# Out products of two slices in one run, in the float32r layers of the groups of 448 columns

## The chip, the cores and the metric

The kernel runs on one core of one Trainium2 chip. The metric is the device time of one execution in microseconds (us), the median of several runs.

## The reference

Attention with a memory, then two gated feed-forward layers ("MoE" by their names, with a single expert). With B = 4, H = 8, S = 576, D = 64:

```python
local = softmax(causal(q @ k.T / sqrt(D))) @ v
mem   = (phi(q) @ M_prev) / (phi(q) @ z_prev + 1e-6)       # phi(x) = elu(x) + 1
x     = g * mem + (1 - g) * local                          # g = sigmoid(beta), by head
x     = x.reshape(B * S, 512)                              # 2304 tokens
xn    = x / sqrt(mean(x * x) + 1e-6) * rms_g
x1    = (silu(xn @ w_gate) * (xn @ w_val)) @ w_out         # 512 -> 1536 -> 512
out   = (sigmoid(x1 @ w_gate2) * (x1 @ w_val2)) @ w_out2
```

All is float32. The kernel reaches that precision by writing each operand as a high and a low part and adding three products (high by high, high by low, low by high).

## The kernel before

The tokens are worked in five groups: group -1 has the first 128 tokens of all four batches (512 columns), groups 0 to 3 have the other 448 tokens of one batch each (448 columns). Each group goes through both layers, l = 0 and l = 1. A layer is cut into 12 slices of 128 hidden units. For a slice f, `hidden` makes two sums in PSUM, `pg` (gate) and `pv` (value), with twelve matmuls each (line 961: four blocks of 128 by three products). `gated` turns them into the hidden values `h`: a tanh on ScalarE (line 981), then on VectorE lines 983 and 986 for a first layer or line 990 for a second, and a split into a high and a low part (lines 998 and 999, or 1005 and 1006). `out_share` multiplies `h` with the out weights into four accumulators `po` (line 1027), twelve matmuls again. `pg` and `pv` come from a pool of two PSUM buffers (`psm`), `h` from three buffers, and `po` stands in four banks for a whole layer.

In group 0 and up the products of `hidden` are made in 16-bit halves (f16), except in the first two slices of a second layer, which are float32r. The out products are float32r in both layers of group 0 and in the first layer of group 1, and f16 halves later on. The rows show float32r operands as f32.

Weights: SyncE loads them from copies kept in DRAM into a ring of thirteen buffers (`slot`; in the rows `ws`, `wl`, `wr`, `wrl`). In the layers of group 0 a slice takes three of them: one for the kept raw weights (line 915), one for their halves, which are made there (`halve`: lines 830 to 837 on ScalarE, GpSimd and VectorE), and one for the out weights (line 927). In group 1 the halves are loaded ready (line 903).

While a group's layers run, the attention of the next group is worked in between in small steps (`att_qk`, `att_scores`, `att_av`, `att_mem`, lines 210 to 638), and in group 1 also the halving of the out weights for later (`share_steps`). After the out products of each slice the loop sets out some of these steps. SyncE issues all loads and stores in one queue, in order; an instruction that waits there holds up those behind it.

The order on each engine is not that of the program: a planner (`schedule_with_timeline_sim=True`) goes through the instructions with priorities in program order and its own times, and gives each engine the next that it takes to be ready. Within an engine the chip then keeps to that order.

The part of the loop that matters here: `hidden(f)` comes first, and the out products of slice f-1 after it, so that `h` of f-1 has had the time of a slice to be made. `done` counts the steps and sets the pace of the attention work.

Of the kernel before, what the change touches and what calls it, by code (L numbers as in the profile page):

```python
# [68 lines left out]
def attn_moe_moe_kernel(ctx, tc, qT, kT, qk0, v, mz, beta, w8, rms_g, outT):  # L69
# [11 lines left out]
    NF = w8.shape[1]  # L81
# [884 lines left out]
    def hidden(w, l, f, n, g, x, h, o=0, home=("mm", "mm")):  # L966

        pool, tag = late[home[0]], home[1]
        pg = pool.tile([128, NMAX], F32, tag=tag, name="pg")
        mm3(pg, w[0], x, n, o)  # L970
        pv = pool.tile([128, NMAX], F32, tag=tag, name="pv")
        mm3(pv, w[1], x, n, o)

        gated(pg, pv, l, f, n, g, h, o)
# [35 lines left out]
    def htiles(g, l, f):  # L1010
        t = wp.tile([128, NMAX], F32, tag="t", bufs=3, name="t")
        if plain(g, l, f):
            return t, None
        if is_share(g, l, f):
            return t, late["h"].tile([128, 2, 2, NMAX], F16, tag="h", bufs=3, name="h")[:, 0]
        return t, late["h"].tile([128, 2, NMAX], F32R, tag="h", bufs=3, name="h")

    def out_share(w, h, po, n, first, last):
        t, hh = h
        low = 0 if hh is None or w[2].shape[1] < 3 else 2  # L1020
        for d in range(KD):
            c = slice(d * 128, (d + 1) * 128)
            if hh is None:
                nc.tensor.matmul(po[d][:, 0:n], w[2][:, c], t[:, 0:n], start=first, stop=last)
                continue
            for i, (a, b) in enumerate(((0, 0), (low, 1), (1, 0))):
                nc.tensor.matmul(  # L1027
                    po[d][:, 0:n], w[2][:, a, c], hh[:, b, 0:n], start=(first and i == 0), stop=(last and i == 2)
                )
# [3 lines left out]
    def token_sums(xh, tag):  # L1033

        t = xp.tile([128, 2, 4, NMAX], F16, tag=tag, name="t" + tag)
        halves = [t[:, a, :, 0:2 * NT].rearrange("p j (k n) -> p j k n", k=2) for a in range(2)]
        for k in range(2):
            x = ap_.tile([128, SW], F32, tag="pt", name="xw")[:, 0:4 * NT].rearrange("p (i n) -> p i n", i=2)
            nc.vector.tensor_tensor(
                out=x,  # L1040
                in0=xh[0].rearrange("p (i k) n -> p k i n", k=2)[:, k, :, 0:2 * NT],
                in1=xh[1].rearrange("p (i k) n -> p k i n", k=2)[:, k, :, 0:2 * NT],
                op=ALU.add,
            )
            part = lambda i, j: x[:, i, j * NT:(j + 1) * NT]
            tw = ap_.tile([128, SW], F32, tag="sc", bufs=2, name="tw")[:, 0:4 * NT].rearrange("p (j n) -> p j n", j=4)
            for j, (a, b) in enumerate(
                ((part(0, 1), part(0, 0)), (part(1, 1), tw[:, 0]), (part(1, 1), part(0, 1)), (tw[:, 1], part(1, 0)))
            ):
                nc.vector.tensor_tensor(out=tw[:, j], in0=a, in1=b, op=ALU.subtract)  # L1050
            nc.scalar.copy(out=halves[0][:, :, k], in_=tw)
            nc.vector.tensor_tensor(out=halves[1][:, :, k], in0=tw, in1=halves[0][:, :, k], op=ALU.subtract)
        return halves
# [301 lines left out]
    def last_of(e):  # L1355
        return next(i for i in reversed(nc.cur_bb.bb.instructions) if i.engine == e)

    def behind(pairs):

        stack = ExitStack()  # L1360
        for pair in pairs:
            for i in pair:
                stack.enter_context(tc.issue_after(i))
        return stack

    def lagged(n):

        return marks[-n:len(marks) - n + 1] if len(marks) >= n else []
# [18 lines left out]
    def unit_slices(g):  # L1387
        mid = NF if g < B - 1 else NF // 2 + 2
        for e, c in ((nc.vector, slice(NWIDE, mid)), (nc.gpsimd, slice(mid, NF))):
            if c.start < c.stop:  # L1390
                e.tensor_scalar(out=unit[2][:, c], in0=unit[1][:, c], scalar1=st["half_is1"], scalar2=None, op0=ALU.mult)
# [45 lines left out]
    for g in range(-1, B):  # L1437
        n = 512 if g < 0 else S - 128
# [16 lines left out]
        for l in range(2):  # L1455
            early = 2 if g < 0 and l == 0 else 0
            ws, hs, halfway = early_ws[:early], early_hs[:early], []
            for f in range(early):
                hidden(ws[f], l, f, 256, g, xt, hs[f], 256, (("mm", "mm"), ("ps", "pa"))[f])
                halfway.append(tuple(last_of(e) for e in (mybir.EngineType.Activation, mybir.EngineType.DVE)))  # L1460
            po = None
            if g == B - 1:
                po = [late[f"po{d // 2}"].tile([128, NMAX], F32, tag=f"po{d}", name="po") for d in range(KD)]
                halves = xt if l == 0 else xh
                xs = token_sums(halves, "c" if l == 0 else "a")
                last_slices(l, n, xt, halves, xs, po)
            for f in range(0 if g == B - 1 else NF + 1):
                if f < NF:
                    if f >= early:
                        if g > 0 and l == 1 and f == NWIDE:  # L1470
                            unit_slices(g)
                        turn = lagged(BACK[g + 1]) if g <= 0 else []
                        if g < 0 and l == 1 and f in (2,):
                            turn = turn + evacuated
                        if g >= 0 and l == 0 and f in (1, 2):
                            turn = turn + tokens_done
                        with behind(turn + (halfway[-1:] if early and f < early + 3 else [])):
                            ws.append(weights(g, l, f))
                        hs.append(htiles(g, l, f))
                        if g == B - 2 and l == 1 and f == NF - 3:  # L1480
                            first_sums(0)
                        hidden(ws[f], l, f, n, g, xh if l == 1 and is_half(g, l, f) else xt, hs[f])
                        marks.append(tuple(last_of(e) for e in (mybir.EngineType.Activation, mybir.EngineType.DVE)))
                if f > 0:
                    if po is None:
                        po = [late[f"po{d // 2}"].tile([128, NMAX], F32, tag=f"po{d}", name="po") for d in range(KD)]
                    out_share(ws[f - 1], hs[f - 1], po, n, f == 1, f == NF)
                    done += 1
                    with ExitStack() as after:

                        if g < 0 and done < 5:
                            traced = nc.cur_bb.bb.instructions
                            for e in (mybir.EngineType.Activation, mybir.EngineType.DVE, mybir.EngineType.SP):
                                after.enter_context(
                                    tc.issue_after(next(i for i in reversed(traced) if i.engine == e))
                                )
                        for step in shares[done]:
                            with behind(lagged(2)):
                                step()
                        while used < len(steps) and used < len(steps) * (done - wait) // (total - wait):  # L1500
                            with behind(lagged(AFTER[g + 1])):
                                steps[used]()
                            used += 1
                            if used == len(steps):
                                tokens_done = [tuple(last_of(e) for e in (mybir.EngineType.Activation, mybir.EngineType.DVE))]
            if g < 0 and l == 0:
                begin.close()
            xn = wide_tokens("cd") if l == 0 else None
            for d in range(KD):
                evacuate(l, d, n, g, po[d], xn)  # L1510
            evacuated = [tuple(last_of(e) for e in (mybir.EngineType.Activation, mybir.EngineType.DVE))]
            if l == 0 and g >= 0:
                xh = half_tokens("b")
                with tc.high_priority(400):
                    halve_tokens(g, n, po, xh)
                    if g >= NSHARE[1]:
                        group_unit()
            if l == 0 and g < 0:
                with tc.issue_after(z["gm"]):
                    token_scale()  # L1520
            xt = xn
# [56 lines left out]
```

## Time and profile before

| | |
|---|---|
| Median of three runs | 1014.85 us (1014.1 to 1015.68) |
| The profiled execution | 1016.42 us |
| Its span, first to last instruction | 1014.6 us |
| TensorE busy | 999.3 us (98%) |
| VectorE busy | 832.1 us (82%) |
| ScalarE busy | 654.7 us (65%) |
| Mean granted clock of TensorE | 0.996 of full speed |

Busy times are sums over the span. The ends of matmuls are modelled: a matmul of 448 columns shows some 0.35 us although one starts every 0.19 us, so the pace is read from one start to the next. PE is TensorE (PEld its weight loads), DVE VectorE, ACT ScalarE, POOL GpSimd, SPq the queue of SyncE. L1027 is line 1027 of the kernel. A granted clock of 1.00 is 2.4 GHz, 0.50 is 1.2 GHz.

### The profile page before, as it was taken

What the parts mean: (1) busy time and instruction counts of PE and PEld (TensorE: products, weight loads), DVE (VectorE), ACT (ScalarE), POOL (GpSimd) and SP (SyncE); (2) the same over time, 40 slices, a digit from 0 to 9 for tenths busy, and PEclk for the clock granted to TensorE, in tenths of its full rate; (3) what the DMA queues carried; (4) which work ended last, traced back from release to release, by engine and by line L of the source; (5) the groups of instructions that cost most, each with busy time, mean ns of one, the idle gap of its engine ahead of it and who ended that gap; (6) DMA issues with size and microseconds to landing.
All of it is one profiled execution on the core that took longest, in us unless ns stands there. A gap on an engine that the chain in (4) does not pass through costs nothing.

```text
span 1014.6 us, 19021 instructions
## 1 busy us (share of the span) xinstructions
PE 999.3 (98%) x6721; PEld 700.0 (69%) x6721; DVE 832.1 (82%) x1826; ACT 654.7 (65%) x1238; POOL 201.8 (20%) x339
## 2 busy tenths in 40 slices
PE   9999999999999999999999999999999999999998
PEld 6878887888666676666666765555567556876885
DVE  6989999997769998775998977757779776995883
ACT  7668887786678888674778676535456353543452
POOL 4203221141004233300424432002133100000000
PEclk9999999999999999999999999999999999999999
DMA  9599998986894676498779856995544256836521
GB/s 350 180 373 398 345 352 257 376 308 200 272 368 172 224 251 229 177 322 240 246 257 322 266 179 224 309 340 167 174 144 167 83 159 212 284 135 226 201 84 37
DMA packets 102561, 243.74 MB, mean 240 GB/s; under 512 B 25154, under 2 KB 37058, under 8 KB 102466
## 3 DMA queue, kind: packets, MB, share of 16 engines
q1 hardware_dynamic: 102322, 242.41, 69.8%
q8 instruction: 53, 0.87, 0.3%
q14 instruction: 42, 0.34, 0.1%
q10 hardware_dynamic: 144, 0.11, 0.0%
HBM read 187.43 MB, written 51.38 MB: 235 GB/s over the span
## 4 chain that ended last, share of the span: by engine, by line
PE 65%; DVE 14%; issue 9%; DMA 6%; ACT 5%; POOL 1%; SPq 0%; DVEq 0%; POOLq 0%; ACTq 0%
PE po L1027 20%; PE pg L961 16%; PE pv L961 15%; PE pw L1137 7%; PE ps L253 2%; DMA qd<-in_qT 1%; PE pm L638 1%; POOL sc L555 1%; DVE mx L572 1%; DMA raw<-in_w 1%; DMA wr<-kept 1%; PE pav L589 1%; PE pav L591 1%; PE pav L590 1%; DVE w L878 1%
## 5 line engine op out<-in xcount | busy, mean ns | idle before, releaser
L555 POOL TENSOR_SCALAR_AFFINE_SELECT sc<-sc 128x128 f32<-128x128 f32 (+1 forms) x128 | 73.0, 583 | 194.1 <-ACT sc L550 193.3
L1027 PE MATMUL po<-h,ws 128*128 128x448 f16 (+2 forms) x468 | 107.6, 375 | 0.0
L961 PEld LDWEIGHTS <-ws 128*128 128x128 f16 x552 | 53.5, 99 | 53.1 <-issue 4.9
L1027 PE MATMUL po<-h,wl 128*128 128x448 f16 (+2 forms) x372 | 86.8, 376 | 0.1
L961 PEld LDWEIGHTS <-wr 128*128 128x128 f16 x552 | 52.8, 98 | 49.2 <-issue 3.5
L1027 PE MATMUL po<-h,wr 128*128 128x448 f16 (+1 forms) x384 | 84.9, 364 | 0.2 <-ACT h L1005 0.2
L574 POOL PARTITION_ALL_REDUCE mb<-mx x32 | 61.3, 1915 | 70.9 <-DVE mx L572 62.1
L981 ACT ACTIVATE t<-pg,unit 128x448 f32<-128x448 f32 x70 | 43.8, 626 | 40.3 <-PE pg L961 40.1
L550 ACT COPY sc<-ps 128x512 f32<-128x512 f32 (+1 forms) x96 | 52.7, 562 | 18.6 <-PE ps L253 18.5
L1027 PEld LDWEIGHTS po<-h,ws 128*128 128x128 f32 x300 | 55.9, 188 | 9.4
L961 PEld LDWEIGHTS <-wl 128*128 128x128 f16 x360 | 34.7, 98 | 31.7 <-issue 1.3
L253 PE MATMUL ps<-qq,kk 128*128 128x64 f16 (+2 forms) x280 | 53.2, 295 | 0.0
L237 ACT ACTIVATE sc<-sc,qs 128x1472 f32<-128x1472 f32 x24 | 36.6, 1526 | 23.4 <-DVE sc L580 15.4
L990 DVE SCALAR_TENSOR_TENSOR t<-t,pv 128x448 f32<-128x448 f32 (+1 forms) x52 | 32.7, 629 | 18.6 <-PE pv L961 18.3
L1027 PEld LDWEIGHTS po<-h,wl 128*128 128x128 f32 x228 | 42.5, 188 | 8.0 <-ACT h L998 0.5
L1027 PE MATMUL po<-h,wrl 128*128 128x448 f16 (+1 forms) x192 | 44.0, 374 | 1.6 <-ACT h L1005 1.4
L983 DVE SCALAR_TENSOR_TENSOR t<-t,pg 128x448 f32<-128x448 f32 (+2 forms) x50 | 30.9, 618 | 15.4 <-ACT t L981 15.3
L872 ACT ACTIVATE top<-raw 128x512 f16<-128x512 bf16 x50 | 38.0, 784 | 5.6 <-DMA raw<-in_w 4.4
L998 ACT CAST h<-t 128x448 fp32r<-128x448 f32 (+1 forms) x46 | 27.0, 586 | 19.6 <-DVE t L986 14.4
L572 DVE TENSOR_TENSOR mx<-mx,sc 128x320 f32<-128x320 f32 (+2 forms) x96 | 34.5, 359 | 4.0 <-POOL sc L555 3.1
L1155 ACT COPY sn<-pw 128x224 f32<-128x224 f32 x54 | 18.2, 341 | 30.0 <-PE pw L1137 27.9
L878 DVE SCALAR_TENSOR_TENSOR w<-raw,top 128x512 int32<-128x512 int32 x48 | 35.3, 747 | 0.8 <-ACT top L872 0.6
(437 smaller groups left out, 2870.0 us busy)
## 6 DMA issues: line engine op xcount, KB each, us to landing
raw<-in_w SPq DMA_DIRECT2D x50, 511.8 KB, 6.4
kept<-w SPq DMA_DIRECT2D x48, 256.0 KB, 5.2
ws<-parts SPq DMA_DIRECT2D x24, 512.0 KB, 5.4
wr<-half SPq DMA_DIRECT2D x23, 512.0 KB, 4.1
rawl<-in_w SPq DMA_DIRECT2D x22, 511.8 KB, 6.5
wr<-parts SPq DMA_DIRECT2D x21, 512.0 KB, 5.6
ws<-half SPq DMA_DIRECT2D x21, 512.0 KB, 4.7
kd<-in_kT SPq DMA_DIRECT2D x64, 144.0 KB, 3.5
```

The lines of the kernel that those rows point to most:

```text
L237: nc.scalar.activation(out=sc, in_=sc, func=AF.Exp, scale=both)
L253: nc.tensor.matmul(ps[:, c0:c0 + n], kk[:, k0:k0 + 128], r[:, q0 - 128:q0 - 128 + n], start=(i == 0), stop=(i == 1))
L550: nc.scalar.copy(out=sc[:, o:o + c], in_=ps[:, 0:c])
L555: nc.gpsimd.affine_select(out=d, in_=d, compare_op=ALU.is_ge, fill=NEG, base=SQ[kt] - T0[kt], pattern=[[1, n]], channel_multiplier=-1,)
L572: nc.vector.tensor_tensor(out=mx[:, q:448], in0=mx[:, q:448], in1=sc[:, d:d + 448 - q], op=ALU.max)
L574: nc.gpsimd.partition_all_reduce(mb[:, 0:448], mx[:, 0:448], channels=128, reduce_op=bass_isa.ReduceOp.max)
L872: nc.scalar.activation(out=top.bitcast(F16).rearrange("p (n t) -> p n t", t=2)[:, :, 1], in_=raw.bitcast(BF16)[:, :, 2], func=AF.Copy)
L878: nc.vector.scalar_tensor_tensor(out=dst.bitcast(I32), in0=raw.rearrange("p n t -> p (n t)").bitcast(I32).rearrange("p (n t) -> p n t", t= ...
L961: nc.tensor.matmul(ps[:, 0:n], w[:, a, k * 128:(k + 1) * 128], x[b][:, k, o:o + n], start=(i == 0), stop=(i == 3 * KD - 1))
L981: nc.scalar.activation(out=t, in_=pg[:, 0:n], func=AF.Tanh, scale=u[:, 0:1] if half else 0.5)
L1027: nc.tensor.matmul(po[d][:, 0:n], w[2][:, a, c], hh[:, b, 0:n], start=(first and i == 0), stop=(last and i == 2))
L1137: nc.tensor.matmul(regions[m][at], left(i, m, a, k), right(j, b, k), start=first and c == 0, stop=c == 5, skip_group_check=True,)
```

## The change

In the three float32r layers of the groups of 448 columns, which are l = 0 and 1 of group 0 and l = 0 of group 1, the out products are no longer set out one slice at a time behind each slice. Behind an odd slice there are none; behind an even slice f those of slices f-2 and f-1 follow one another. The last pair, of slices 10 and 11, comes at the layer's end, where there is no further slice. The steps of attention are set out at the same counts as before.

```diff
@@ -1484,7 +1484,9 @@
                 if f > 0:
                     if po is None:
                         po = [late[f"po{d // 2}"].tile([128, NMAX], F32, tag=f"po{d}", name="po") for d in range(KD)]
-                    out_share(ws[f - 1], hs[f - 1], po, n, f == 1, f == NF)
+                    by_two = g in (0, 1) and l <= 1 - g
+                    for i in ((f - 2, f - 1) if f % 2 == 0 else ()) if by_two else (f - 1,):
+                        out_share(ws[i], hs[i], po, n, i == 0, i == NF - 1)
                     done += 1
                     with ExitStack() as after:
```

## Rows read from the trace of the kernel before

**Rows 1.** The page: span, TensorE's busy time, and the chain of waits by engine.

```profile
span 1014.6 us, 19021 instructions
...
PE 999.3 (98%) x6721; PEld 700.0 (69%) x6721; DVE 832.1 (82%) x1826; ACT 654.7 (65%) x1238; POOL 201.8 (20%) x339
...
PE 65%; DVE 14%; issue 9%; DMA 6%; ACT 5%; POOL 1%; SPq 0%; DVEq 0%; POOLq 0%; ACTq 0%
```

**Rows 2.** Sums by stretch, the three layers: length, busy us by engine, clock, DMA.

```profile
264.00:364.00 100.00, 98.69 (x627) 64.91 (x627) 85.92 (x187) 78.00 (x168) 23.91 (x47) 1.00 0.79 274
364.00:472.00 108.00, 105.98 (x724) 72.97 (x723) 82.56 (x207) 76.45 (x159) 21.75 (x46) 0.98 0.72 239
472.00:567.00 95.00, 94.08 (x650) 63.67 (x647) 87.55 (x210) 72.69 (x132) 32.47 (x54) 1.00 0.80 268
```

**Rows 3.** TensorE's timeline, undisturbed slices: start us, us, engine, line, form, count.

```profile
444.00 2.44 PE L961 MATMUL pg<-hb,wl 128*128 128x448 f16 x12
446.28 2.43 PE L961 MATMUL pv<-hb,wl 128*128 128x448 f16 x12
448.39 2.76 PE L1027 MATMUL po<-h,wl 128*128 128x448 f32 x12
450.99 2.44 PE L961 MATMUL pg<-hb,wr 128*128 128x448 f16 x12
...
458.01 1.31 PE L961 MATMUL pg<-hb,wrl 128*128 128x448 f16 x6
```

**Rows 4.** TensorE's timeline where a pg starts; in brackets what it waited for.

```profile
317.75 2.43 PE L961 MATMUL pg<-ha,ws 128*128 128x448 f16 x12 [0.69 <-DVE t L983]
...
343.46 0.74 PE L961 MATMUL pg<-ha,wrl 128*128 128x448 f16 x3
...
479.89 0.35 PE L961 MATMUL pg<-ha,wr 128*128 128x448 f16 x1
...
495.62 2.43 PE L961 MATMUL pg<-ha,ws 128*128 128x448 f16 x12 [0.27 <-DVE t L983]
...
512.97 1.29 PE L961 MATMUL pg<-ha,wr 128*128 128x448 f16 x6 [0.65 <-DVE t L983]
```

**Rows 5.** TensorE's timeline at the end of group 0's first layer.

```profile
358.27 3.61 PE L1027 MATMUL po<-h,ws 128*128 128x448 f32 x16
```

**Rows 6.** The timeline of TensorE's weight loads beside rows 3.

```profile
448.36 2.41 PEld L1027 LDWEIGHTS po<-h,wl 128*128 128x128 f32 x12
```

**Rows 7.** VectorE's timeline: the readers of pg in first layers.

```profile
340.97 0.62 DVE L983 SCALAR_TENSOR_TENSOR t<-t,pg 128x448 f32<-128x448 f32 x1
...
477.47 0.61 DVE L983 SCALAR_TENSOR_TENSOR t<-t,pg 128x448 f32<-128x448 f32 x1
...
494.96 0.61 DVE L983 SCALAR_TENSOR_TENSOR t<-t,pg 128x448 f32<-128x448 f32 x1
...
512.30 0.61 DVE L983 SCALAR_TENSOR_TENSOR t<-t,pg 128x448 f32<-128x448 f32 x1
```

**Rows 8.** ScalarE's timeline: the reader of a pg in the second layer.

```profile
449.72 0.61 ACT L981 ACTIVATE t<-pg,unit 128x448 f32<-128x448 f32 x1
```

**Rows 9.** TensorE's timeline, group 0's second layer, before slice 7.

```profile
425.53 0.67 PE L1027 MATMUL po<-h,wrl 128*128 128x448 f32 x2 [1.37 <-ACT h L1005]
426.48 3.71 PE L1027 MATMUL po<-h,wrl 128*128 128x448 f32 x10 [0.28 <-DVE h L1006]
429.99 0.75 PE L961 MATMUL pg<-hb,ws 128*128 128x448 f16 x2
```

**Rows 10.** Sums by stretch, columns as in rows 2.

```profile
427.00:430.30 3.30, 3.30 (x10) 2.49 (x9) 3.11 (x13) 3.16 (x8) 0.34 (x2) 0.50 0.00 0
```

**Rows 11.** The timeline of SyncE's queue.

```profile
413.53 0.33 SPq L915 DMA_DIRECT2D wr<-kept  x1
430.21 0.33 SPq L915 DMA_DIRECT2D wrl<-kept  x1
```

**Rows 12.** VectorE's timeline: the last halving of slice 11's weights.

```profile
450.00 0.74 DVE L837 SCALAR_TENSOR_TENSOR wrl<-wrl,s 128x512 f16<-128x512 f32 x1
```

## The prediction, made before the change was run

> **What bounds the kernel now.** I read the page first: its busy times and its chain of waits. TensorE is busy 999.3 of 1014.6 us, and it holds 65% of the chain that ended last; no other engine holds more than 14% [rows 1]. Then the sums by stretch, for the three layers that the change touches: the first and second layer of group 0 (264 to 364 us and 364 to 472 us) and the first layer of group 1 (472 to 567 us). I write them (0,0), (0,1) and (1,0). In them TensorE is busy 98.7 of 100, 106.0 of 108 and 94.1 of 95 us. VectorE is busy 85.9, 82.6 and 87.6 us [rows 2]. So TensorE sets the time, and VectorE, at 92% in (1,0), has little room to be late. TensorE's idle time in the three is 1.3 + 2.0 + 0.9 = 4.2 us: more than that no better order can win, save what a low clock costs.
>
> Third, the timeline of TensorE where nothing disturbs it. One slice is twelve matmuls for pg, twelve for pv, both in 16 bits, and twelve out products (po) in 32 bits. Twelve 16-bit matmuls take 446.28 - 444.00 = 2.28 us, 0.190 us each. The out products show a start of 448.39, just inside the last pv matmul, and the next pg starts at 450.99: 2.60 us, of which some 0.16 is the rest of that pv matmul, so 0.203 us each [rows 3]. The reader is to see that these runs touch each other without a hole.
>
> Fourth, who holds the next slice back. Two PSUM buffers serve pg and pv in turn, so the pg of slice f+1 needs the pg of slice f read. In a first layer the last reader is line 983 on VectorE, in a second layer line 981 on ScalarE. Where the reader is late TensorE waits: 0.69, 0.27 and 0.65 us at three places [rows 4].
>
> **The change, part by part.** No instruction is added or removed. In each of the three layers the out products of an even slice, twelve matmuls, move behind the next-but-one slice's pg and pv. The order h0 o h1 h2 o h3 o (h a slice's pg and pv, o an out run) becomes h1 h2 o o h3 h4 o o.
>
> *Fewer changes of type.* Out products of slices 10 and 11 already run one after the other at a layer's end; a run of sixteen stands there [rows 5]. So five joins a layer are new, fifteen in all. What does a change from 16 to 32 bits and back cost? A whole slice lasts 450.99 - 444.00 = 6.99 us or 458.01 - 450.99 = 7.02 us. Its matmuls make 24 x 0.190 + 12 x 0.203 = 7.00 us. So the cost of a change to and fro lies between 0 and about 0.03 us. The first 32-bit weight load starts at 448.36, in front of its matmul, while the last 16-bit one still streams; the twelve loads fill 2.41 us, 0.20 us each [rows 6], which is the pace of the products within a run too, and a longer run does not change it. I take 0.02 x 15 = **0.3 us won** (bounds 0 and 0.45).
>
> *Cover lost after odd slices.* Work done before an odd slice's pg is the same as now. After it, no out run follows, so TensorE asks for the next pg 2.6 us earlier. There are five such places a layer (slices 1, 3, 5, 7, 9). The room now is the start of the next pg less the end of its reader [rows 3, 4, 7, 8]:
> (0,0) slice 9: 343.46 - (340.97 + 0.62) = 1.87 us, 0.73 short of 2.6.
> (0,1) slice 9: 450.99 - (449.72 + 0.61) = 0.66, 1.94 short.
> (1,0) slice 1: 479.89 - (477.47 + 0.61) = 1.81, 0.79 short.
> (1,0) slice 3: 495.62 - (494.96 + 0.61) = 0.05, 2.55 short.
> (1,0) slice 5: 512.97 - (512.30 + 0.61) = 0.06, 2.54 short.
> At the other ten I found at most 0.3 us missing. Within a layer these don't add up: VectorE is held there by its own queue of attention work, not by TensorE, so a TensorE that has once waited 2.55 us comes later to the next such place by as much. The delay of a layer is nearest to its largest shortfall: 0.73 + 1.94 + 2.55 = 5.2 us. That is the upper end. The lower end is nothing: the order on each engine is written by a planner that works with its own times, and where it sees the pg buffer taken it can put an out product, ready since the slice before, into the hole; now it has none left to put there. Its foresight is not perfect, or the three waits of today would have been filled from elsewhere. Neither end is nearer by a row, so I take the middle, **2.6 us lost**.
>
> *Cover won after even slices.* An even slice's pg starts 2.6 us earlier against the same next pg. The wait of 0.69 us at 317.75 follows an even slice, 6 [rows 4]. Its reader stands in VectorE's queue for other work, so I count nothing; the other bound is 0.7 won.
>
> *Buffers held longer.* The three h buffers cost nothing: the buffer that slice f+1 takes was read by the out products of f-2, which in both orders stand before slice f+1's pg. The PSUM banks of po are read once a layer, behind the same last product. The buffers of out weights of even slices are freed a slice later. In the layers of group 0 a slice takes three of thirteen buffers in turn, so the buffer of slice f's out weights is that into which slice f+5's kept weights are loaded. The cover is those slices of lead; what happens when it is gone is the fourth rival.
>
> Sum: -0.3 + 2.6 = **+2.3 us**. The profiled execution took 1016.42 us around its span of 1014.6, and the sum against it gives 1018.7. It was 1.6 us over the median of the runs, 1014.85; against that the sum gives **1017.2 us**.
>
> What a wait costs beyond itself: after waits of 1.37 and 0.28 us at 424 to 426.5 the granted clock was 0.50, the lower of the two levels, from 427.0 to 430.3 us [rows 9, 10]. The ten products from 426.48 to 429.99 took 3.51 us in place of 10 x 0.203, so 1.5 us were lost. The waits of 0.69 us and less left the clock at 1.00 [rows 2, 4]. If the shortfalls of 2.55 and 1.94 us come whole, each may bring 1.5 us more: 5.2 + 3.0 - 0.3 = +7.9, or 1022.8 us.
>
> **The rivals.** *The holes are filled and nothing is left* (chance 0.31). The planner breaks up the double runs, or VectorE's queue comes out in another order. For it: it mixes single out products with other matmuls already, and the run of sixteen at 358.27 shows it joining runs unasked [rows 5]. Against it: the three waits. Time: the 0.3 us alone, 1014.5.
>
> *Faster* (0.22). In (0,1) the wait at 424 to 430 costs 1.37 + 0.28 + 1.5 = 3.15 us: the out products of slice 6 were pulled in front of slice 7, whose weights were late, and waited for their own h (line 1005 on ScalarE). With the change these products come later in the program, behind slice 8, when h is long there. If TensorE then finds slice 7 ready, or other work, 3.15 + 0.3 are won, and 0.7 more with the wait at 317.75: 1014.85 - 4.15 = 1010.7 us. It decides if slice 7's weights are ready within 1.4 us of TensorE's reaching them; against it, pg of slice 7 started only at 429.99 although nothing of TensorE's stood before it but these products.
>
> *A buffer freed late* (0.07). The load at 430.21 into the buffer `wrl` stood on SyncE's queue from 413.86, until slice 6's last out product was done at 429.99, and all loads behind it stood too [rows 9, 11]. If those products come two slices later, 14 us (458.01 - 444.00), the load starts near 444.2. Its weights were halved 450.74 - 430.21 = 20.5 us after it started [rows 12], which gives 464.7 against slice 11's pg at 458.01: 6.7 us of wait and 1.5 of clock, 1023.0 us. It decides from a delay of 458.01 - 450.74 = 7.3 us.
>
> *Short waits lower the clock too* (0.04). If the clock fell at all five places even where the wait is partly filled, 5 x 1.5 is added: 1014.85 + 2.3 + 7.5 = 1024.6. The three short waits of today speak against it. The Trainium skill, "TensorE: Matmul & The Clock Gate", section "A second HAM failure mode: psum-queue depth-cycling", tells of a kernel in which short idles between groups of matmuls, from going round PSUM banks, made the clock swing between its two levels and cost throughput; it is a rule against this change, and the granted clock here does not bear it out for waits of up to 0.69 us.
>
> **How the numbers follow.** The forecast, some shortfalls left over, has 0.36: from 1016.9 to 1021 us. Filled 0.31, faster 0.22, late buffer 0.07, clock 0.04. About 0.2% (2.0 us) is what a measurement of this kernel can tell from no change. Slower by more: 0.36 + 0.07 + 0.04 = 0.47; within: 0.31; faster by more: 0.22. The range goes from the faster case, 1011, to the whole shortfalls with their clock and the late buffer, 1023.
>
> **What the profile would show.** Right: on TensorE's timeline pg pv pg pv and then 24 out products in one run, with a pace of still 0.203 us; waits of pg for line 983 or 981 of more than the present 1.6 us in total (0.69 + 0.27 + 0.65), above all in (1,0), after odd slices. Wrong: out products spread singly between pg and pv; those waits unchanged; a time under 1013 with the low clock at 427 gone; or long waits of TensorE for weights, with SyncE's queue standing at line 915 longer than 16 us. The prediction fails most easily through the planner: if its order on VectorE or on the load queue is another, waits of several microseconds can appear or go anywhere in the three layers, and none of my rows shows them.

## The result, and the profile after

The changed kernel took 1019.99 us (median of 6 runs, 1016.76 to 1020.89), the kernel before 1013.8 (1011.56 to 1015.68): a ratio of 1.0061, 95% interval 1.0044 to 1.0079. A second measurement, below, gave 1.0076. So it is slower, by 6 to 8 us of 1014. The profiled execution took 1016.76 us around a span of 1015.0 and was the shortest of its six. The page of after, its span, busy times and chain of waits, the lines that answer to [rows 1]:

```profile
span 1015.0 us, 19035 instructions
...
PE 997.0 (98%) x6721; PEld 697.6 (69%) x6721; DVE 835.7 (82%) x1826; ACT 653.1 (64%) x1238; POOL 201.2 (20%) x339
...
PE 69%; DVE 10%; issue 7%; DMA 6%; ACT 5%; POOL 2%; SPq 1%; POOLq 0%; ACTq 0%; DVEq 0%
```

TensorE is still the bound. The sums by stretch of after, columns as in [rows 2], with the stretch behind the three layers as a fourth:

```profile
264.00:364.00 100.00, 98.83 (x627) 64.77 (x625) 85.72 (x187) 78.14 (x169) 25.06 (x48) 1.00 0.79 274
364.00:472.00 108.00, 105.38 (x731) 72.56 (x730) 85.55 (x210) 76.68 (x160) 22.22 (x45) 1.00 0.74 239
472.00:567.00 95.00, 92.97 (x641) 62.21 (x640) 86.24 (x208) 73.38 (x132) 34.05 (x55) 1.00 0.80 269
567.00:600.00 33.00, 29.94 (x225) 21.90 (x225) 30.52 (x78) 23.27 (x46) 11.43 (x22) 1.00 0.51 176
```

TensorE's idle time is 1.2, 2.6 and 2.0 us in the three layers (1.3, 2.0 and 0.9 in [rows 2]), and 3.1 us in the 33 us that follow, where the change touches nothing. TensorE's timeline of after, a place where two slices do run together; it answers to [rows 3]:

```profile
421.10 2.79 PE L1027 MATMUL po<-h,wr 128*128 128x448 f32 x12
423.73 2.59 PE L1027 MATMUL po<-h,wrl 128*128 128x448 f32 x12
426.16 0.61 PE L253 MATMUL ps<-qq,kk 128*128 128x320 f16 x4
```

Twelve products take 426.16 - 423.73 = 2.43 us, 0.203 each, the pace of before. But such places are few. Counted over the whole traces, the 504 out products in f32 and 448 columns stand in 54 unbroken runs in before and 57 in after; 24 runs of twelve became 17, and two runs of 24 were made. Of the fifteen odd slices that should have no out products behind them, fourteen still have some and nine all twelve (twelve slices had all twelve in before): the planner holds products of a slice back and puts them there.

### The profile page after: what moved, and what is told of

The parts are those of the page before. It is cut to its first block, busy times and chain, and to the rows that moved or that the text cites. A ratio compares the mean times of both kernels' runs of the same rounds, so it can differ in the third digit from the quotient of the medians.

```text
span 1015.0 us, 19035 instructions
## 1 busy us (share of the span) xinstructions
PE 997.0 (98%) x6721; PEld 697.6 (69%) x6721; DVE 835.7 (82%) x1826; ACT 653.1 (64%) x1238; POOL 201.2 (20%) x339
## 4 chain that ended last, share of the span: by engine, by line
PE 69%; DVE 10%; issue 7%; DMA 6%; ACT 5%; POOL 2%; SPq 1%; POOLq 0%; ACTq 0%; DVEq 0%
PE po L1027 21%; PE pg L961 17%; PE pv L961 17%; PE pw L1137 7%; PE ps L253 2%; PE pm L638 1%; PE pav L589 1%; PE pav L591 1%; PE pav L590 1%; DMA ws<-kept 1%; POOL sc L555 1%; DMA qk<-in_qk 1%; DMA out_T<-o 1%; DMA mzt<-in_mz 1%; POOL mb L574 1%
## 5 line engine op out<-in xcount | busy, mean ns | idle before, releaser
L555 POOL TENSOR_SCALAR_AFFINE_SELECT sc<-sc 128x128 f32<-128x128 f32 (+1 forms) x128 | 69.8, 558 | 193.0 <-ACT sc L550 192.3
L574 POOL PARTITION_ALL_REDUCE mb<-mx x32 | 63.6, 1986 | 71.0 <-DVE mx L572 57.3
L575 DVE TENSOR_TENSOR sc<-sc,mb 128x896 f32<-128x896 f32 x32 | 34.8, 1087 | 2.3 <-POOL mb L574 2.2
```

Of the source, the lines that this page charges most:

```text
L555: nc.gpsimd.affine_select(out=d, in_=d, compare_op=ALU.is_ge, fill=NEG, base=SQ[kt] - T0[kt], pattern=[[1, n]], channel_multiplier=-1,)
L574: nc.gpsimd.partition_all_reduce(mb[:, 0:448], mx[:, 0:448], channels=128, reduce_op=bass_isa.ReduceOp.max)
L575: nc.vector.tensor_tensor(out=two, in0=two, in1=mb[:, None, 0:448].to_broadcast([128, 2, 448]), op=ALU.subtract)
```

## The experiments

**Both kernels again**, to see what one execution is worth. No edit.

> The kernel before, unchanged, to see how its executions differ among themselves. If the low clock at 427 us and the wait of TensorE for slice 6's h at 424 us belong to every execution, the spans are near 1014.6 us with a mean clock of 0.996. If they come and go (the executions timed so far reach from 1011.6 to 1015.7 us), some executions show a span near 1010 us with a mean clock of 0.998 or more, and the profile taken here may lack them: then the first profile of the kernel before was one of its slow executions, and its difference of 0.4 us to the first profile of the changed kernel hides most of the loss of 6 us.

Measured: 1012.55 us, ratio 1.0003 (0.999 to 1.0017). Its profile has a span of 1010.9 us; the first one of the same program had 1014.6. The wait of 1.37 us before slice 7 and the low clock behind it [rows 9, 10] are not in it; from slice 6 to slice 7 of that layer they make 2.7 of the 3.7 us between the spans. Nor is a second stretch of low clock, which the first profile has at slice 2 of layer (1,1), the second layer of group 1. There TensorE waits about as long in both profiles, 1.84 and 1.67 us, but in the first the twelve matmuls behind the wait took 587.37 - 583.43 = 3.94 us in place of 2.28, another 1.7 us:

```profile
583.43 4.13 PE L961 MATMUL pg<-hb,ws 128*128 128x448 f16 x12 [1.84 <-DMA ws<-half]
587.37 2.45 PE L961 MATMUL pv<-hb,ws 128*128 128x448 f16 x12
```

Both stretches belong to an execution and not to the kernel.

> The changed kernel, unchanged. Its first profile (span 1015.0 us, clock 0.999) was its fastest of six; the others had spans of 1015.8 to 1019.1 us and clocks of 0.997 or 0.998. Theory of the planner: TensorE's order is nearly that of before, the loss lies in waits for loads (the transposed tokens at 465 us, the weights at 583 us), and a slower execution adds a low clock behind one of them: some 1.5 us for each 3.4 us at half clock. Theory of the lost cover: a slower execution shows more waits of pg for lines 983 and 981 than the 1.7 us of the first profile. Time 1017 to 1021 us by both.

Measured: 1019.62 us, ratio 1.0076 (1.0053 to 1.0099), span 1017.8. Where TensorE waits, in the second profile of before (who waits, for what, us in total, times, longest):

```profile
PE pg L961 <- DVE t L983: 1.9, 2, 1.2
PE pg L961 <- DMA ws<-half: 1.7, 1, 1.7
...
PE pg L961 <- ACT t L981: 0.5, 2, 0.3
PE pg L961 <- DMA ha<-x: 0.5, 1, 0.5
```

and in the first profile of after:

```profile
PE pg L961 <- DMA ws<-half: 2.9, 1, 2.9
PE pg L961 <- DMA ha<-x: 1.9, 2, 1.3
PE pg L961 <- DVE t L983: 1.8, 4, 0.7
...
PE pav L589 <- ACT top L246: 0.9, 1, 0.9
PE pm L638 <- DVE shared L766: 0.9, 1, 0.9
...
PE pg L961 <- ACT t L981: 0.7, 3, 0.3
```

The waits for the readers of pg, lines 983 and 981 (those of [rows 4]), are 2.4 us in before and 2.5 in after (2.1 and 2.7 in the other profile of each): what the forecast rests on hardly grew. What grew stands at four places of TensorE's timeline of after, the two largest of them waits for loads:

```profile
466.66 2.44 PE L961 MATMUL pg<-ha,ws 128*128 128x448 f16 x12 [1.34 <-DMA ha<-x]
...
543.97 2.43 PE L961 MATMUL pg<-ha,ws 128*128 128x448 f16 x12 [0.70 <-DVE t L983]
...
563.99 0.68 PE L638 MATMUL pm<-mzt,ph 128*128 128x130 f32 x4 [0.87 <-DVE shared L766]
...
585.49 2.44 PE L961 MATMUL pg<-hb,ws 128*128 128x448 f16 x12 [2.88 <-DMA ws<-half]
```

The first is the start of (1,0), whose transposed tokens (ha) come late. The second is a piece of cover lost: it stands behind slice 9 of (1,0), which has one out product behind it in after and twelve in before. It is made up for at slice 7 of (0,0), where the wait for line 983 is 0.52 us in place of 1.25. The last is slice 2 of layer (1,1). The second profile of before waits at the last place alone (1.67 us). Against it the four are 1.3 + 0.7 + 0.9 + 1.2 = 4.1 us, as much as lies between the spans (1015.0 - 1010.9); what differs elsewhere, slice 7 of (0,0) among it, comes out even. From there to the end the two executions keep their distance. In the second profile of after the last wait was longer, and twelve matmuls behind it took 590.55 - 586.58 = 3.97 us in place of 2.28:

```profile
586.58 4.13 PE L961 MATMUL pg<-hb,ws 128*128 128x448 f16 x12 [3.88 <-DMA ws<-half]
590.55 1.68 PE L961 MATMUL pv<-hb,ws 128*128 128x448 f16 x8
```

The sum by stretch at that place, columns as in [rows 2], has a granted clock of 0.52, near the lower level; 1.7 us more were lost. The mean clock of the single executions suggests that this is the common case: it is 0.998 or less in eleven of the twelve executions of after, and 0.999 in the one that was profiled first. The place in the second profile:

```profile
586.60:590.00 3.40, 3.40 (x10) 1.45 (x11) 1.52 (x9) 0.00 (x0) 0.00 (x0) 0.52 0.37 143
```

**The pairs enforced.** The out products are bound to follow the last matmul of the slice before them in the program, so that the planner can't put them earlier.

```diff
                         hidden(ws[f], l, f, n, g, xh if l == 1 and is_half(g, l, f) else xt, hs[f])
+                        last_pv = last_of(mybir.EngineType.PE)
...
-                        out_share(ws[i], hs[i], po, n, i == 0, i == NF - 1)
+                        with tc.issue_after(last_pv) if by_two and f < NF else ExitStack():
+                            out_share(ws[i], hs[i], po, n, i == 0, i == NF - 1)
```

> The change with the order enforced: both out runs of a pair may be issued only after the last pv matmul of the slice in front of them, so that the planner can't put them back. This is what the prediction costed. Theory of the lost cover: 24 out products in one run at a pace of 0.203 to 0.206 us, waits of pg after odd slices of 3 to 5 us in all, with low clock up to 8 us: 1016 to 1022 us, against 1012 to 1015 for the kernel before. Theory that the joined runs pay (0.02 to 0.03 us a join) and the cover suffices: within 1 us of the kernel before. Theory of the planner: the waits for loads depend on the order of the load queue and not on the pairs, so the time can lie on either side, and the profile shows waits for loads at other places than in the changed kernel.

Measured: 1029.3 us, ratio 1.0171 (1.0147 to 1.0194), span 1025.8. Eight runs of 24 f32 products stand in the trace, and 42 runs in all; none of the fifteen odd slices has out products behind it. Its longest waits:

```profile
PE pg L961 <- DVE t L983: 4.3, 4, 1.5
PE ps L253 <- ACT sc L550: 3.7, 3, 1.6
PE pg L961 <- ACT ws L836: 3.4, 1, 3.4
PE pg L961 <- ACT t L981: 2.8, 4, 1.8
```

This is the lost cover, where it is not filled: lines 983 and 981 cost 7.1 us in place of 2.4, 4.7 more. Behind odd slices the largest of them follow slice 9 of (0,0), slice 3 of (0,1) and slices 3 and 5 of (1,0). Their sizes are not those of the forecast (0.73, 2.55 and 2.54 us at the first and the last two), and the second stands where it named none:

```profile
343.02 0.35 PE L961 MATMUL pg<-ha,wrl 128*128 128x448 f16 x1 [1.54 <-DVE t L983]
...
402.31 0.54 PE L961 MATMUL pg<-hb,wl 128*128 128x448 f16 x2 [1.85 <-ACT t L981]
...
502.98 0.35 PE L961 MATMUL pg<-ha,ws 128*128 128x448 f16 x1 [0.79 <-DVE t L983]
...
520.18 0.35 PE L961 MATMUL pg<-ha,wr 128*128 128x448 f16 x1 [0.93 <-DVE t L983]
```

And it is not all: attention's scores (line 550) and the halving of weights (line 836) now come late as well, 7.1 us more that the forecast did not have.

**One layer alone.** The test of the layer is cut to (0,0).

```diff
-                    by_two = g in (0, 1) and l <= 1 - g
+                    by_two = (g, l) == (0, 0)
```

> The change in the first layer of group 0 alone. In the first profile of the changed kernel TensorE's order in this layer is almost that of before and the layer ends 0.3 us later. Theory of the planner: the loss arises later (364 to 590 us), where the load queue is in another order, so this kernel is within 2 us of the kernel before unless its own load order later on is shifted; no pairs form. Theory of the lost cover: 0.7 us of wait at most, after slice 9.

Measured: 1016.47 us, ratio 1.0047 (1.0029 to 1.0065). That is some 4 us more than before, where the lost cover allowed 0.7 and the planner's theory 2, unless loads moved later on. They did: TensorE waits 2.9 us for ha at the start of (1,0), a layer and 100 us behind the one that was changed. Later, with what the next runs had shown, (1,0) alone:

```diff
-                    by_two = g in (0, 1) and l <= 1 - g
+                    by_two = (g, l) == (1, 0)
```

> The change in layer (1,0) alone; in layers (0,0) and (0,1) out products follow each slice as in before. Theory A (each layer's rearrangement costs at the layer's own end, so that the parts add up): of after's 6 us beyond before, (0,0) alone took 3.6, so that this one takes 2 to 3 us at the waits for L983 and shared between 540 and 566 us and at ws from half near 583: 1014.5 to 1016.5 us, ratio 1.002 to 1.004. Theory E (any new order of the planner costs some 4 us or more, since the order of before is a good one among many and the late load is hit by all of them): 1016 to 1020 us, ratio 1.004 to 1.008, with the wait for ws from half longer than 2.5 us.

Measured: 1018.63 us (12 runs, 1015.51 to 1025.55), ratio 1.0046 (1.003 to 1.0063). Its profile is its shortest execution, with a wait of 2.3 us for ws from half, a little under the 2.5 that theory E had named. The time is in theory E's range and above theory A's. The two parts make 0.47 + 0.46 = 0.93%, and the whole change 0.61 to 0.76, with the third layer not yet counted. The intervals are about 0.2% to either side of each, so that the parts seem not to add up, which speaks for theory E but is not shown.

**The order of the other engines, exchanged.** Only TensorE's instructions are moved by the diff, but the planner writes all engines' orders anew: 39 of SyncE's 660 instructions and 154 of VectorE's 1826, counted as the fewest that must be moved to turn one order into the other, stand elsewhere in after. Here each of the two programs gets the order that the other has on SyncE, VectorE, ScalarE and GpSimd, as a chain of dependences without semaphores at the end of the program; the lists are ranks in program order.

```diff
+    orders = {
+        mybir.EngineType.SP: (
...
+        ),
...
+    for engine, order in orders.items():
...
+        for a, b in zip(at, at[1:]):
+            tc.add_manual_dep(
+                own[b],
+                own[a].name,
+                mybir.DependencyInfo(mybir.DependencyClass.NoSync, mybir.DependencyReason.DATA),
+                reason="order",
+            )
```

> The changed kernel, with the instructions of SyncE, VectorE, ScalarE and GpSimd chained in the order that they have in the kernel before (an order alone, no waits). TensorE's order is then the planner's again, from the changed program: 127 runs of out products at 448 columns where before has 122 and after 126. Theory A (the loss came from the order that the planner gave to the other four engines, and so from the times of their loads and evictions): the loss goes, 1011.5 to 1014.5 us, ratio 0.998 to 1.002, and the wait for ws at the second layer of group 1, 2.9 us in after's profile, is under 2.2 us. Theory B (the loss comes from where TensorE's own out products stand): 1017 to 1021 us, ratio 1.004 to 1.008, with the order of the others changing nothing.

Measured: 1018.45 us, ratio 1.0052 (1.0036 to 1.0068). Theory A falls in the form that it had: the order of before on four engines does not give its time back. The time is in theory B's range; the last run of this section tests that.

> The mirror: the kernel before, with the instructions of SyncE, VectorE, ScalarE and GpSimd chained in the order that they have in the changed kernel; TensorE is planned from the program before, out products after every slice. Theory A: the loss is there without the change, 1017 to 1021 us, ratio 1.004 to 1.008, with waits of 2.5 us or more for ws at the second layer of group 1. Theory B: 1011.5 to 1014.5 us, ratio 0.998 to 1.002.

Measured: 1022.12 us, ratio 1.0083 (1.007 to 1.0097). Theory A's side, and a little slower than after itself.

The same edit with the list of SyncE alone, in both programs:

```diff
+    orders = {
+        mybir.EngineType.SP: (
...
+        ),
+    }
```

> The changed kernel, with SyncE's instructions alone (the loads and stores on its queues, 39 of 660 of which stand elsewhere in after) chained in the order of the kernel before. The planner places the rest anew. Theory A1 (it is the place of the loads in SyncE's queue): 1011.5 to 1014.5 us, ratio 0.998 to 1.002. Theory A2 (the loads are late because what they wait for, evictions and copies on VectorE and ScalarE, is late): the queue's order alone gives back at most half, 1015 to 1020 us, ratio 1.003 to 1.008.

Measured: 1023.89 us, ratio 1.0098 (1.0077 to 1.0119). Neither A1 nor A2 had this.

> The kernel before, with SyncE's instructions alone chained in the order of the changed kernel (39 of 660 stand elsewhere; 19 of VectorE and 32 of TensorE move along). Theory A1: 1017 to 1021 us, ratio 1.004 to 1.008. Theory A2 and theory B: at most half of the loss, 1012 to 1016 us, ratio 0.999 to 1.003.

Measured: 1018.75 us, ratio 1.0056 (1.0042 to 1.0069), as A1 said. But four exchanges that are all slower, whichever half they take from before, don't point at an engine. They may point at something that every new mixture hits. All four profiles have a wait for ws from half at slice 2 of (1,1), of 5.6, 3.3, 2.9 and 3.2 us, where before has 1.7. The longest is in the run that has all orders of before but TensorE's; its timeline of TensorE:

```profile
587.61 3.98 PE L961 MATMUL pg<-hb,ws 128*128 128x448 f16 x12 [5.55 <-DMA ws<-half]
```

Why is that load late? SyncE's queue in the second profile of before:

```profile
562.07 0.34 SPq L628 DMA_DIRECT2D ph<-in_qT  x1
564.42 0.32 SPq L778 DMA_DIRECT2D out<-wr  x1
...
568.06 0.32 SPq L903 DMA_DIRECT2D wr<-half  x1
...
576.57 0.58 SPq L903 DMA_DIRECT2D ws<-half  x1
```

and in the first profile of after:

```profile
564.71 0.33 SPq L628 DMA_DIRECT2D ph<-in_qT  x1
...
571.63 0.32 SPq L778 DMA_DIRECT2D out<-wr  x1
575.29 0.32 SPq L903 DMA_DIRECT2D wr<-half  x1
...
579.13 0.58 SPq L903 DMA_DIRECT2D ws<-half  x1
```

What SyncE's queue of after waits for, between 560 and 582 us:

```profile
SPq L778 <- DVE wr L772: 3.6, 1, 3.6
SPq L903 <- DMA out<-wr: 3.3, 1, 3.3
```

The load for slice 2 is issued behind that for slice 3 (in before also behind that for slice 4). In front of it stands a store of halved out weights, which waits for VectorE's line 772; behind the store a load into the buffer that is being stored; then weights and the attention's inputs. Line 772 ran at 563.62 us in before and 570.83 in after. What was held behind the store then goes out close together: in after nine loads are issued between 575.2 and 579.9 us, in before the same nine are spread over 568.0 to 576.6. The load for slice 2 is only 2.6 us later than in before, and TensorE comes to it 2.9 us later (585.49 - 2.88 = 582.61 against 581.40 - 1.67 = 579.73); what makes the wait longer is the time from its issue to its landing. That is, in the second profile of before and the first of after (the second of after has 7.4):

```profile
DMA to landing us min/median/max: 4.8/4.8/4.8
...
DMA to landing us min/median/max: 6.3/6.3/6.3
```

The DMA engines' busy share was 0.85 from 575 to 581 us in that profile of before, and 1.03 from 579 to 585 us in after. That the loads issued together slow each other is read from this; no run tried it by itself.

The load for slice 2 needs none of what stands before it. If its buffer is free when ph goes out, it could go out right behind it; the next runs try that.

**That one load moved.** All five engines are chained in the order that they have in after; in SyncE's list the load (rank 438) goes from behind the inputs of attention to behind ph (rank 442).

```diff
-            "... 439 442 440 425 445 500 446-447 501-503 438 449-450 ..."
+            "... 439 442 438 440 425 445 500 446-447 501-503 449-450 ..."
```

> The changed kernel with all five engines chained in the order that they have in it, and one load moved: the one that brings the hidden weights of slice 2 of layer (1,1) (ws from half) is issued nine places earlier on SyncE, right behind ph from in_qT, whose place in the profile of after is 564.7 us where the load itself went out at 579.1; its buffer is free by then. Theory C (in after the end of group 1's layers waits for this load, which stands in SyncE's queue behind stores and loads that wait for VectorE and TensorE): the wait for it, 2.9 us in one profile of after and 3.9 with 3.4 us of low clock behind it in the other, goes; 1014.5 to 1017.5 us, ratio 1.002 to 1.005. Theory D (the load is only the last of several equally late things, or something next in line takes its place, so that the time stays): 1018 to 1021 us, ratio 1.005 to 1.008, with a wait of the same length on another line between 575 and 595 us.

Measured: 1014.32 us (12 runs), ratio 0.9998 (0.9986 to 1.001). More than theory C asked for: a kernel that was 0.6 to 0.8% slower than before is level with it. TensorE's matmuls stand in the same order as in after, and of the other engines' orders the place of this load alone is another. The mean clock is 0.999 or 1.0 in ten of the twelve executions. In the profile a part of the gain is lost again, much as in theory D but later than it said: after's profile does not have this wait for VectorE's line 717, 40 us behind slice 2:

```profile
625.63 0.46 PE L638 MATMUL pm<-mzt,ph 128*128 128x130 f32 x2 [1.30 <-DVE inv L717]
```

The same move in before:

```diff
-            "... 439 442 425 440 445-447 500-501 449 502-503 438 450 ..."
+            "... 439 442 438 425 440 445-447 500-501 449 502-503 450 ..."
```

> The same move in the kernel before: all five engines chained in the order of before, and the load of ws from half for slice 2 of layer (1,1) issued ten places earlier on SyncE, right behind ph from in_qT (562.1 us in the profile of the second run of before, where the load itself went out at 576.6). Theory C: the wait of 1.7 to 1.8 us for it goes, and with it the low clock that followed it in the first profile: 1009 to 1012 us, ratio 0.997 to 0.999. Theory D: 1012 to 1014 us, ratio 0.999 to 1.001.

Measured: 1011.29 us (12 runs), ratio 0.9972 (0.9958 to 0.9987), as theory C said. In its profile the load goes out at 562.52 us. SyncE's queue there:

```profile
562.13 0.34 SPq L628 DMA_DIRECT2D ph<-in_qT  x1
562.52 0.42 SPq L903 DMA_DIRECT2D ws<-half  x1
```

and TensorE's slice 2, which shows no wait:

```profile
580.14 2.44 PE L961 MATMUL pg<-hb,ws 128*128 128x448 f16 x12
```

Last, the changed program with the other engines in the order of before, as above, and with the load moved in the same way. Against before with the same move only TensorE's order is another.

```diff
-            "... 439 442 425 440 445-447 500-501 449 502-503 438 450 ..."
+            "... 439 442 438 425 440 445-447 500-501 449 502-503 450 ..."
```

> The changed kernel with the other four engines in the order of the kernel before, as in the run after_rest_as_before, all five engines chained in the order that they had there, and the load of ws from half for slice 2 of layer (1,1) moved ten places earlier on SyncE, behind ph from in_qT. Against the kernel before with the same move, TensorE's own order (some 46 matmuls that stand elsewhere, out products of two slices joined where the planner left them so) is the one thing that is different. Theory C (that run lost 5.6 us at this load, 5.55 us of wait and the low clock behind it, less 1.8 that before waits too): 1010.5 to 1013 us, ratio 0.997 to 1.000, and the joins themselves are worth less than 1 us either way. Theory B (TensorE's own order costs): 1014 to 1017 us, ratio 1.001 to 1.004, with waits elsewhere in its stead.

Measured: 1010.74 us (9 runs), ratio 0.9969 (0.9957 to 0.9982). That run had been at 1.0052; this load and what hung on it were the whole of its loss, and theory B falls. Against before with the same move (0.9972) the new order of TensorE in this run is worth nothing that can be measured. It is not that of after, though: chained to the other engines' old order the planner moved few matmuls, and the trace has 59 runs of f32 out products and none of 24. So it says that these few moves cost nothing, and nothing on what a join is worth. These two versions beat both kernels.

## Why the prediction was right in its number and wrong in its cause

The time came out 2.8 us over the forecast, in its range and on the likeliest side; against the kernel before, 1013.8 us over its six runs, it is 6.2 us where 2.3 were forecast. The sum that led there did not hold: its largest term came to almost nothing, and the 6 to 8 us came by ways that had no price in it. That both make the kernel slower by a few us is luck.

*Fewer changes of type, 0.3 us won.* The pace within a run, 0.203 us, held to the digit. Few of the fifteen joins were made, and no run shows by itself what one is worth: the enforced pairs make them, but lose much else.

*Cover lost after odd slices, 2.6 us lost: this is the step that failed.* As built, waits for lines 983 and 981 went from 2.4 to 2.5 us. The lower end of that term, nothing, was nearest: the prediction said that the planner has no out product left to put behind an odd slice. It keeps one slice's products back and puts a run there as before; the cover failed at one place, slice 9 of (1,0), for 0.7 us. (The order that the prediction writes out for before is a slip: the loop has h0 h1 o h2 o h3 o. The rows were read by the right one.) Where the pairs were enforced, the same two waits grew by 4.7 us, near the upper end of 5.2, but place by place they do not agree: 1.54 us at slice 9 of (0,0) where 0.73 was read, none at slice 9 of (0,1) where 1.94 was, but 1.85 at slice 3, and 0.79 and 0.93 at slices 3 and 5 of (1,0) where 2.55 and 2.54 were. The room read in one order is not the room in another, and the agreement of the sums is luck. The rest of that run's loss, some 12 of 17 us (1.71% of 1013), was not in the sum.

*What stood in its place.* Under the planner's new order VectorE's line 772 comes 7.2 us later, and with it the store and the loads behind it on SyncE's queue; the load for slice 2 of (1,1), put behind them and issued among them, held TensorE 1.2 to 2.2 us longer than in before (2.88 and 3.88 against 1.67), in one of the two profiles with low clock behind it, 1.7 us more. That the load is the cause is shown by moving it. That line 772 is the way to it is read from the profiles of after, and it is not the only one: with the four engines in the order of before the store goes out at 568.85 us, the load for slice 2 still at 581.04, and TensorE waits 5.55 us. Moving it takes the ratio from 1.0061 and 1.0076 to 0.9998 in after, and from 1 to 0.9972 in before. The move wins 0.63 to 0.78% in after, 6.4 to 7.9 us, and 0.28% in before, 2.8 us: the difference, 3.6 to 5.1 of the 6 to 8 us lost, is what the change had added at this load. The layer lies outside the three that I had looked at. The prediction named this way to fail in its last sentences, but gave it no price.

*What is left.* With the load moved in both, after is still 3.0 us slower (1014.32 - 1011.29). The two profiles show 2.5 us between the spans. The waits that only after's has are 1.2 us for ha at the start of (1,0), 0.7 for line 983 at the place of 543.97, 0.9 for line 766 at that of 563.99 and the 1.3 for line 717; before's has shorter ones of its own. No run tried these by themselves, so that part is read from the profiles and stays open.

*The rivals.* "The holes are filled and nothing is left" had the planner right and the time wrong (1014.5): it counted TensorE's order and not those of the others. "Faster" rested on the wait before slice 7 [rows 9], which the second profile of before doesn't have; in such an execution there was nothing to win. "A buffer freed late" did not come: the only wait for weights over 0.3 us in the first profile of after is that of (1,1). "Short waits lower the clock too": the granted clock of the three layers of after is 1.00, with waits of up to 1.34 us in them. The rule of the Trainium skill, "TensorE: Matmul & The Clock Gate", section "A second HAM failure mode: psum-queue depth-cycling", on idles between groups of matmuls is borne out by no run here for waits as short as those that it was weighed against, 0.69 us and less; nearest to it comes a place in the run with enforced pairs, at the end of this document.

## What to carry to other kernels

Where a planner writes the order, as here, a diff to one engine is a diff to all: before costing the edit, ask whether the planner can undo it, and read which loads and stores will be issued in another place. A load that TensorE already waits for, here 1.7 us, is where a new order can lose most: seven of the eight new orders tried here, with the load not moved, wait longer for it than before. Look in its queue for what stands in front of it that it does not need; moving it won 2.8 us in before, where the change's forecast had counted on 0.3. And read a wait in two profiles of the same program before building a gain on it.

## What the runs showed of the hardware that was not expected

The same instruction order took spans of 1014.6 and 1010.9 us in two profiles: 2.7 us of it at one wait of 1.37 us and the low clock behind it, and 1.7 us at low clock behind a wait of 1.84 us; 0.7 us went the other way before that.

How long TensorE had waited at once did not decide whether its clock fell. After 1.84 us it was 0.57 (first profile of before, 583.5 to 587 us); at the same place of the second, after 1.67 us, it was 1.00. After 2.88 us (after, 585.5 to 589.5 us) and after 3.38 us (the enforced pairs, 435 to 439 us) the granted clock was 1.00; after 3.88 us it was 0.52. In the run with enforced pairs it fell at 580 us, where waits of 1.11 us (until 578.92) and 1.09 us (until 580.69) stood close together. Sums by stretch, columns as in [rows 2], of before (first profile), of after (first profile), and two of that run:

```profile
583.50:587.00 3.50, 3.50 (x11) 1.45 (x12) 3.10 (x13) 2.30 (x4) 1.94 (x4) 0.57 0.40 134
...
585.50:589.50 4.00, 4.00 (x22) 2.08 (x23) 2.52 (x12) 2.15 (x3) 0.00 (x0) 1.00 0.47 180
...
435.00:439.00 4.00, 3.71 (x19) 1.79 (x20) 3.39 (x5) 4.00 (x8) 0.00 (x0) 1.00 0.40 133
...
580.00:583.40 3.40, 2.71 (x8) 2.25 (x8) 3.40 (x8) 1.17 (x3) 0.68 (x3) 0.55 0.71 202
```
